# Gated stage: the next load of x ahead of the stores of prepared parts; first expert: units in pairs

## The chip, the core and the metric

The kernel runs on one core of a Trainium2 chip. The metric is the device time of one execution, in microseconds (us), as the median of several runs. The engines are TensorE (PE in the profile: matmuls; PEld: their weight loads), VectorE (DVE), ScalarE (ACT), GpSimd (POOL) and SyncE (SP), whose queue here issues all loads and stores of the stages that matter below.

## The reference

Three stages follow each other. Attention over keys and values that are averaged by eights gives x (2304 rows of 512). Four experts with relu, weighted by given probabilities, turn it into a new x. A gated block multiplies two projections, and two more matrices follow.

```python
k_p = k.reshape(B, H, Sp, 8, D).mean(axis=3)          # v_p likewise
attn = softmax(scale * q @ k_p.T)                     # exp, sum, divide
x = (attn @ v_p) as (2304, 512)
p = domain_probs / (domain_probs.sum(-1) + 1e-09)
for e in range(4):
    h = np.maximum(x @ w1[e], 0.0)                    # 512 -> 1024
    out += p[:, e:e + 1] * (h @ w2[e])                # 1024 -> 512
x = out
h = (x @ g_w1) * (x @ g_w2) @ g_w3
result = h @ g_wout
```

All of it is in float32.

## The kernel before, in words

Each product is made of three matmuls, since each operand is split into a rounded high part and the rest (`mm3`, lines 173 to 175; `hi_lo`, lines 178 and 179). Rounded means that ScalarE copies the operand into a type of fewer bits, and VectorE or GpSimd subtracts the copy from the operand.

**First expert.** It runs over six blocks of 384 rows and, in each, over eight slices of 128 hidden columns: 48 units. A unit has a first product (`expert_h`: x times w1, 12 matmuls of 384 columns into one PSUM bank, called F below) and a second product (h times w2, 9 matmuls of 512 columns into three banks, called S). Two banks alternate for first products (`g1_bank`). ScalarE applies the relu (line 688) and VectorE takes the rest (line 689), and these two hidden tiles sit in rings of `LAG + 1` places until the second product, `LAG` = 2 units later, has read them. The order of the work is the order in which this code is written: `run_units` writes F of unit n, a gap of attention pieces (`between(2 * n)`), S of unit n - 2, and another gap (`between(2 * n + 1)`). The pieces of the gaps (scores, exponentials, sums, normalisation, transposes, the product with v, loads) prepare x for the later blocks; which gap takes which piece is a table (`hooks`, `also`). The product with v (`attend`, line 557, tile x_ps) takes four banks, two of them the ones that alternate for first products.

**Gated stage.** It goes twice (`half`) over three batches of 768 rows. A batch has four rounds of seven products (`gated_rows`, `seven`: 168 matmuls of 384 columns, tile s) and then second products (72 matmuls of 512 columns, tile g). In the first half, while a batch runs, the x of the next batch is prepared (`prepare_x`): it is loaded into a buffer (`load_x`, line 775, tile xr, which lies in the area x5h), two ScalarE copies make high parts (lines 905 and 906), VectorE the rest and the sums, and at the end four stores per part are put on the list `stores` (line 918, to `kept`). `put_away` issues what is on that list. One buffer serves all these loads, so the load of the next x waits until the last preparation has read it. `give` copies a finished tile out of PSUM with ScalarE (line 1402) and stores it (line 1403, tile half). In the round that follows, ScalarE first makes the copies of the newly loaded x (`prepare_x(0, ...)`) and then copies the first of the seven products out of PSUM (line 961), on which VectorE's additions and the release of the banks depend.

Of the kernel before, what the change touches and what calls it, by code (L numbers as in the profile page):

```python
# [17 lines left out]
def fused_kernel(  # L18
# [23 lines left out]
    E, _, F = moe_w1.shape  # L42
    P = 128
# [8 lines left out]
    FC = F // P  # L52
# [16 lines left out]
    LAG = 2  # L69
# [41 lines left out]
    def row(base, at, size, bufs):  # L111
        return Ring(base, [at + size * n for n in range(bufs)])
# [13 lines left out]
    ZT = 2 * BS * 4  # L126
    XO = 7 * HALF_ROW
    EXTRA = 2 * P * 4
# [5 lines left out]
    H0 = 2 * FC * ROW  # L134
    HT = XT // KC

    def area(tag, size, dtype, name):
        return home.tile([P, size // 4], dtype, tag=tag, name=name)
# [3 lines left out]
    round_ = area("round", (FC - 1) * ZT + 2 * EXTRA, F32R, "round")  # L142
# [1 line left out]
    acc_a = Places(acc=Ring(plain, [WORK]))  # L144
    dp = plain[:, :NTILE * E].rearrange("p (t e) -> p t e", e=E)
    w1pool = Places(w1h=row(round_, 0, ROW, FC), w1l=row(round_, FC * ROW, ROW, FC))
    hpool = Places(hh=row(round_, H0, HT, LAG + 1), hl=row(round_, H0 + (LAG + 1) * HT, HT, LAG + 1))
    dpool = ctx.enter_context(tc.tile_pool(name="dpool", bufs=1, space=bass.MemoryType.DRAM))
    ps_q = ctx.enter_context(tc.tile_pool(name="ps_q", bufs=1, space=PSUM))
    ps_p = ctx.enter_context(tc.tile_pool(name="ps_p", bufs=KC, space=PSUM))  # L150
# [21 lines left out]
    def mm3(ps, lh, ll, rh, rl, first, last):  # L172
        nc.tensor.matmul(ps, lh, rl, start=first, stop=False)  # L173
        nc.tensor.matmul(ps, ll, rh, start=False, stop=False)  # L174
        nc.tensor.matmul(ps, lh, rh, start=False, stop=last)  # L175
# [62 lines left out]
    class Rounding:  # L238
# [35 lines left out]
        def step(self, most):  # L274
            self.load()
            if self.steps == most:
                self.flush()
                return
            self.steps += 1
            r, sink = self.loaded.pop(0)  # L280
            a = dec.tile([P, HALF], F32, tag="store")
            au = a.bitcast(U32)
            l, h = r[:, :, 0], r[:, :, 1]
            low = r.bitcast(F32)[:, :, 0]
            nc.vector.tensor_scalar(au, h, 0x7FFFFFFF, None, op0=ALU.bitwise_and)  # L285
            nc.vector.tensor_scalar(h, h, 0x80000000, None, op0=ALU.bitwise_and)
            nc.vector.tensor_scalar(a, a, LEAST, MOST, op0=ALU.max, op1=ALU.min)
            self.flush()
            nc.vector.scalar_tensor_tensor(au, au, 3, h, op0=ALU.logical_shift_left, op1=ALU.bitwise_xor)
            nc.vector.tensor_scalar(low, l, 2.0 ** -51, 2.0, op0=ALU.mult, op1=ALU.add)  # L290
            nc.gpsimd.tensor_tensor(au, au, l, op=ALU.add)  # L291
            self.done = a, sink
# [37 lines left out]
    with tc.manual_schedule():  # L330
# [60 lines left out]
        def cooled(most):  # L391
            while cooling and cooling[0][0] <= most:
                _, kind, spot = cooling.pop(0)
                spots[kind].append(spot)
# [180 lines left out]
        def fetch(most=None, only=None):  # L575
            for what in loads[:most]:
                if spots[kind_of(what)] and (only is None or what in only):
                    loads.remove(what)
                    {"q": load_q, "qb": load_qb, "k": load_k, "v": load_v}[what[0]](*what[1:])

        def do(piece):
            what, f = piece
            f()
            if what:
                done(what)
# [61 lines left out]
        at = {TPB: 0, TPB + 1: 5, TPB + 2: 8}  # L647
# [123 lines left out]
        def load_x(b, kc):  # L771
            r = late["small"].tile([P, 2, 2, HB], F32, tag="xr", name="xr", bufs=2)
            for n in range(2):
                rows = turned_d[(kc + 2 * n) * P:(kc + 2 * n + 1) * P]
                nc.sync.dma_start(r[:, n], rows[:, b * BS:(b + 1) * BS].rearrange("p (a s) -> p a s", a=2))
            xr_t[kc] = r
# [143 lines left out]
        def put_away():  # L920
            for f in stores:
                f()
            stores.clear()
# [64 lines left out]
        def between(n):  # L988
            clock[0] = n + 1
            cooled(n - 1)  # L990
            fetch(2)
            if n < len(hooks):
                for piece in hooks[n]:
                    do(piece)

        units = [("e", (0, i), fc) for i in range(NB) for fc in range(FC)]
        w_units = [("w", (b,), fc) for b in range(len(w3_blocks)) for fc in range(FC)]

        def make(u):
            kind, key, fc = u  # L1000
            return {"e": expert_h, "w": w3_h}[kind](*key, fc)

        def weights(u):
            kind, key, fc = u
            if kind == "e":
                return w2_t[key[0], fc]
            return wo_t[fc]

        def finish(u, pss):
            kind, key, fc = u  # L1010
            {"e": accumulate, "w": keep_w34}[kind](*key, pss)

        def rows(u):
            return w3_blocks[u[1][0]][1] if u[0] == "w" else TPB
# [3 lines left out]
        FIRST = ATT_BLOCKS * FC + 4  # L1018
        also = {}
# [24 lines left out]
        def made(u):  # L1044

            kind, key, fc = u
            if kind == "e":
                e, i = key
                if i == 0:
                    if fc + LAG < FC:  # L1050
                        stream.split(nc.vector)
                    stream.split()
            else:
                n = key[0] * FC + fc
                for f in early.get(n, ()):
                    f()
# [10 lines left out]
        def met(u):  # L1067

            kind, key, fc = u
            if kind == "e":  # L1070
                e, i = key
                if i == NB - 1:
                    stream.split()


        def add_pair(e, j):
            for fc in (j, j + NJ):
                stream.add(moe_w1[e, :, fc * P:(fc + 1) * P].rearrange("(k p) f -> p k f", p=P), (KC, P))

        def refill_first():  # L1080
            for n in range(FIRST, NB * FC + LAG):
                if n in at_pairs:
                    add_pair(1, at_pairs[n])
                if n >= NB * FC + LAG - FC:
                    add_w2(1, turn_of[n - (NB * FC + LAG - FC)])
            for j in range(len(at_pairs), NJ):
                add_pair(1, j)
# [36 lines left out]

        hs = {}

        def run_units(units, lo, hi):
            for n in range(lo, hi):
                if n < len(units):
                    u = units[n]  # L1130
                    hs[n] = make(u)
                    made(u)
                    if u[0] == "e":
                        if n == FIRST:
                            refill_first()
                        between(2 * n)
                        for f in also.get(2 * n, ()):
                            f()
                if n >= LAG:
                    u = units[n - LAG]  # L1140
                    fc = u[2]
                    if fc == 0:
                        n_out = rows(u)
                        pss[:] = [(bank_p if u[0] == "e" else bank_r)("g2") for _ in range(n_out)]
                    hh, hl = hs.pop(n - LAG)
                    wh, wl = weights(u)
                    for o, ps in enumerate(pss):
                        sl = slice(o * P, (o + 1) * P)
                        mm3(ps, hh[:, sl], hl[:, sl], wh[:, 0], wl[:, 0], fc == 0, fc == FC - 1)
                    if fc == FC - 1:  # L1150
                        finish(u, pss)
                    met(u)
                if n < len(units) and units[n][0] == "e":
                    between(2 * n + 1)
                    for f in also.get(2 * n + 1, ()):
                        f()

        pss = []
        run_units(units, 0, len(units) + LAG)

        def take_x():
            xo_t.update(xo_next)
# [174 lines left out]
        for half in range(2):  # L1337
            for n_b, b in enumerate(g_order):
# [3 lines left out]
                make = half == 0 and not swap  # L1342
# [77 lines left out]
                for m in range(len(tiles)):  # L1420
                    js = range(NJ) if last and m >= 2 else [NJ - 1]
                    if last and m == len(tiles) - 1:
                        for cols in pieces:
                            run(m, js, cols)
                            give_part(m, cols)
                        break
                    run(m, js)
                    give(m)
                    if swap and m == 2:
                        weights_of(2)  # L1430
                    if m == 1:
                        put_away()
                if half == 0 and n_b < BN - 2:
                    load_x(g_order[n_b + 2], 0)
                if not last:
                    spare_slot = second
                    take_x()
# [35 lines left out]
```

## Time and profile before

| | |
|---|---|
| median of 3 runs | 1164.74 us (1164.29 to 1164.87) |
| the profiled execution | 1164.62 us |
| its span, first to last instruction | 1162.9 us |
| PE busy | 1144.2 us, 98% of the span |
| PEld busy | 1035.3 us, 89% |
| DVE busy | 792.1 us, 68% |
| POOL busy | 423.5 us, 36% |
| ACT busy | 370.0 us, 32% |
| DMA, read and written | 213.85 MB, mean 184 GB/s |

The profile page also cuts the span into 40 equal slices of 29.07 us and gives the busy tenths of each engine in each, with the granted clock of TensorE. Where a slice of the busiest engine falls below 9 tenths, the chain of waits (the work that ended last, followed back step by step) says what it waited for. A timeline lists instructions in order of time; "x4" at the end of a row means that four were merged into it, and the bracket gives the idle time of the engine ahead of it and what ended that. SyncE's rows (SPq) show the time that issuing a DMA took, and not the transfer. A busy TensorE is not necessarily a fast one, so the start-to-start distance of matmuls is read as well.

### The profile page before, as it was taken

To read this page: it belongs to the slowest core of one execution; us is meant where nothing else is said; L and a number is where in the kernel's file an instruction comes from. 1 tells how busy PE (TensorE), PEld (TensorE's weight loads), DVE (VectorE), ACT (ScalarE), POOL (GpSimd) and SP (SyncE) were. 2 spreads that over 40 slices of the span, in tenths; PEclk is the share of its full clock that TensorE was granted. 3 is DMA by queue.
4 is the path that set the end of the run, shared out by engine and by line. 5 is a ranking of instruction groups with operands and counts; after the bars stand their busy time and mean duration, and the time that the engine had idled before them with its cause. 6 is when DMAs were issued, how large, how long until landed. Compare 5 with 4: busy or idle time off the path is not lost.

```text
span 1162.9 us, 17117 instructions
## 1 busy us (share of the span) xinstructions
PE 1144.2 (98%) x5966; PEld 1035.3 (89%) x5966; DVE 792.1 (68%) x1464; ACT 370.0 (32%) x615; POOL 423.5 (36%) x393
## 2 busy tenths in 40 slices
PE   8999999999999999999999999999999979999998
PEld 6888898999989898989898989899889979999997
DVE  6867553767768598748679568786786545774554
ACT  4543433345313053504043512225352213230110
POOL 6975212424615166624336643424001011331211
PEclk9999999999999999999999999999999989999999
DMA  8866424364876726496944588875475344947341
GB/s 220 198 155 144 159 83 163 153 196 177 293 246 188 237 78 184 145 293 201 261 135 118 169 258 201 244 180 179 120 182 203 143 156 176 340 167 269 120 168 55
DMA packets 213766, 213.85 MB, mean 184 GB/s; under 512 B 88880, under 2 KB 169008, under 8 KB 213680
## 3 DMA queue, kind: packets, MB, share of 16 engines
q1 hardware_dynamic: 213392, 212.23, 58.3%
q8 instruction: 47, 0.77, 0.3%
q10 hardware_dynamic: 288, 0.52, 0.1%
q14 instruction: 39, 0.32, 0.1%
HBM read 140.87 MB, written 71.83 MB: 183 GB/s over the span
## 4 chain that ended last, share of the span: by engine, by line
PE 90%; issue 3%; DMA 3%; DVE 2%; SPq 1%; ACT 1%; POOL 1%; POOLq 0%; DVEq 0%; ACTq 0%
PE g L174 17%; PE g L175 17%; PE g L173 17%; PE s L173 12%; PE s L175 12%; PE s L174 12%; PE x_ps L557 1%; PE sc L503 1%; DMA raw<-in_moe_w_dram 1%; PE at_ps L542 1%; POOL round L179 0%; DMA x5h<-turned 0%; SPq L1403 0%; DVE ap L418 0%; DMA plain<-gate 0%
## 5 line engine op out<-in xcount | busy, mean ns | idle before, releaser
L957 DVE TENSOR_TENSOR plain<-s,plain 128x384 f32<-128x384 f32 x300 | 158.2, 554 | 90.6 <-ACT plain L961 39.3
L179 POOL TENSOR_TENSOR round<-x5l,round 128x768 fp32r<-128x768 f32 x60 | 112.3, 1871 | 282.2 <-ACT round L178 247.8
L173 PE MATMUL s<-xo,wh 128*128 128x384 f32 x624 | 209.0, 335 | 0.0
L175 PE MATMUL s<-xo,wh 128*128 128x384 f32 x624 | 209.0, 335 | 0.0
L174 PE MATMUL s<-xo,wl 128*128 128x384 f32 x624 | 208.9, 335 | 0.0
L173 PE MATMUL g<-w2l,round 128*128 128x512 f32 x522 | 204.4, 392 | 0.0
L175 PE MATMUL g<-w2h,round 128*128 128x512 f32 x522 | 204.1, 391 | 0.0
L174 PE MATMUL g<-w2h,round 128*128 128x512 f32 x522 | 203.9, 391 | 0.0
L173 PEld LDWEIGHTS s<-xo,wh 128*128 128x128 f32 x624 | 117.6, 188 | 0.5
L174 PEld LDWEIGHTS s<-xo,wl 128*128 128x128 f32 x624 | 117.5, 188 | 0.5
L175 PEld LDWEIGHTS s<-xo,wh 128*128 128x128 f32 x624 | 117.4, 188 | 0.0
L175 PEld LDWEIGHTS g<-w2h,round 128*128 128x128 f32 x522 | 98.0, 188 | 20.7
L173 PEld LDWEIGHTS g<-w2l,round 128*128 128x128 f32 x522 | 98.1, 188 | 19.6 <-issue 0.8
L174 PEld LDWEIGHTS g<-w2h,round 128*128 128x128 f32 x522 | 98.0, 188 | 19.0
L291 POOL TENSOR_TENSOR x5l<-x5l,x5h 128x256 uint32<-128x256 uint32 x80 | 60.5, 757 | 139.6 <-DVE x5h L290 132.9
L961 ACT ACTIVATE plain<-s 128x384 f32<-128x384 f32 x60 | 29.2, 487 | 230.9 <-PE s L175 195.1
L178 ACT ACTIVATE round<-x5l 128x768 fp32r<-128x768 f32 x60 | 50.9, 848 | 146.1 <-DVE x5l L1332 145.0
L179 POOL TENSOR_TENSOR round<-plain,round 128x768 fp32r<-128x768 f32 (+1 forms) x29 | 52.3, 1805 | 115.3 <-ACT round L178 86.6
L285 DVE TENSOR_SCALAR x5l<-x5h 128x256 uint32<-128x256 uint32 x80 | 50.5, 632 | 54.7 <-DMA gate<-x5l 31.1
L957 DVE TENSOR_TENSOR x5l<-s,plain 128x384 f32<-128x384 f32 x120 | 65.2, 555 | 24.3 <-PE s L175 17.8
L689 DVE SCALAR_TENSOR_TENSOR round<-g,round 128x384 fp32r<-128x384 f32 x48 | 26.4, 553 | 62.9 <-ACT round L688 62.7
L173 PE MATMUL g<-xl,round 128*128 128x384 f32 x192 | 66.6, 347 | 0.0
(240 smaller groups left out, 2215.4 us busy)
## 6 DMA issues: line engine op xcount, KB each, us to landing
xo<-keptx SPq DMA_DIRECT2D x42, 768.0 KB
raw<-in_moe_w_dram SPq DMA_DIRECT2D x64, 256.0 KB
keptx<-xo SPq DMA_DIRECT2D x12, 768.0 KB
x5h<-in_moe_w_dram SPq DMA_DIRECT2D x128, 64.0 KB
x5h<-in_moe_w_dram SPq DMA_DIRECT2D x32, 256.0 KB
ob<-acc SPq DMA_DIRECT2D x24, 256.0 KB
kept<-xo SPq DMA_DIRECT2D x8, 768.0 KB
xo<-kept SPq DMA_DIRECT2D x8, 768.0 KB
```

Source lines behind the costliest of these rows:

```text
L173: nc.tensor.matmul(ps, lh, rl, start=first, stop=False)
L174: nc.tensor.matmul(ps, ll, rh, start=False, stop=False)
L175: nc.tensor.matmul(ps, lh, rh, start=False, stop=last)
L178: nc.scalar.activation(hi, src, AF.Copy)
L179: (lo_eng or nc.vector).tensor_tensor(lo, src, hi.bitcast(F32), op=ALU.subtract)
L285: nc.vector.tensor_scalar(au, h, 0x7FFFFFFF, None, op0=ALU.bitwise_and)
L291: nc.gpsimd.tensor_tensor(au, au, l, op=ALU.add)
L503: nc.tensor.matmul(sc[off:off + n, (hp % 2) * W:(hp % 2 + 1) * W], qT[:, hp, off:off + n], kT_t[b][:, hp * W:(hp + 1) * W], start=True, st ...
L542: nc.tensor.transpose(pt[:NK, g * P:(g + 1) * P], e[:, half * G + g, :], ident)
L689: nc.vector.scalar_tensor_tensor(hl, ps, 0.0, hh.bitcast(F32), op0=ALU.max, op1=ALU.subtract)
L957: nc.vector.tensor_tensor(to, one, two, op=ALU.add)
L961: nc.scalar.activation(x, product(j, A11, B11), AF.Copy)
```

## The change

In the gated stage, `put_away` is no longer called after the second finished tile of a batch but after all six, and behind the load of x for the batch after the next one. In the first expert the first eight units run as before; from the ninth on, two units go together: two first products, then two second products, with the same numbered gaps behind each of the four. The rings of hidden tiles have four places in place of three. The rest of `run_units` serves the later weight products as before.

```diff
-    hpool = Places(hh=row(round_, H0, HT, LAG + 1), hl=row(round_, H0 + (LAG + 1) * HT, HT, LAG + 1))
+    hpool = Places(hh=row(round_, H0, HT, LAG + 2), hl=row(round_, H0 + (LAG + 2) * HT, HT, LAG + 2))
...
+        def begin_unit(units, n):
+            if n < len(units):
+                u = units[n]
+                hs[n] = make(u)
+                made(u)
+
+        def end_unit(units, n):
...
         def run_units(units, lo, hi):
             for n in range(lo, hi):
...
+                begin_unit(units, n)
+                end_unit(units, n - LAG)
+
+        def run_first():
+
+            def gap(at):
+                if at >= 2 * len(units):
+                    return
+                between(at)
+                for f in also.get(at, ()):
+                    f()
+
+            n, total = 0, len(units) + LAG
+            while n < total:
+                few = 1 if n < FC else 2
+                if n == FIRST:
+                    refill_first()
+                steps = [lambda m=m: begin_unit(units, m) for m in range(n, n + few)]
+                steps += [lambda m=m: end_unit(units, m - LAG) for m in range(n, n + few)]
+                for k, step in enumerate(steps):
+                    step()
+                    gap(2 * n + k)
+                n += few
...
-        run_units(units, 0, len(units) + LAG)
+        run_first()
...
-                    if m == 1:
-                        put_away()
                 if half == 0 and n_b < BN - 2:
                     load_x(g_order[n_b + 2], 0)
+                put_away()
```

On SyncE, at the end of the first gated batch: before, seven of the eight stores of prepared parts (kept), four of the six finished tiles (half), and the load of x (x5h from turned; the row merges it with the batch's later load).

```order
L918 DMA kept<-round 128x1536
L918 DMA kept<-round 128x1152
L918 DMA kept<-z_2637 128x1536
L918 DMA kept<-xo 128x1152
L918 DMA kept<-xo 128x1536
L918 DMA kept<-xo 128x1152
L918 DMA kept<-xo 128x1536
L1403 DMA half_8070<-ob 128x512
L1403 DMA half_8071<-ob 128x512
L1403 DMA half_8072<-ob 128x512
L1403 DMA half_8073<-ob 128x512
L775 DMA x5h<-turned 128x768 x4
```

On SyncE at the same place in the changed kernel (its lines are numbered one to nineteen higher).

```order
L1422 DMA half_8069<-plain 128x512
L1422 DMA half_8070<-ob 128x512
L1422 DMA half_8071<-ob 128x512
L1422 DMA half_8072<-ob 128x512
L1422 DMA half_8073<-ob 128x512
L776 DMA x5h<-turned 128x768 x2
L919 DMA kept<-round 128x1152
L919 DMA kept<-round 128x1536
L919 DMA kept<-round 128x1152
L919 DMA kept<-z_2637 128x1536
```

The load of x stands ahead of all eight stores, and so do the four half stores that stood behind them.

On TensorE, between units 46 and 47 of the first expert (g1 is the bank of a first product, g2 those of a second one): before, the end of one first product, a second product, and the beginning of the next first one.

```order
L175 MATMUL g1_2524<-xh_1910,round_71 128x384
L173 MATMUL g2_2390<-w2l_635,round_71 128x512
L174 MATMUL g2_2390<-w2h_634,round_71 128x512
L175 MATMUL g2_2390<-w2h_634,round_71 128x512
L173 MATMUL g2_2391<-w2l_635,round_71 128x512
L174 MATMUL g2_2391<-w2h_634,round_71 128x512
L175 MATMUL g2_2391<-w2h_634,round_71 128x512
L173 MATMUL g2_2392<-w2l_635,round_71 128x512
L174 MATMUL g2_2392<-w2h_634,round_71 128x512
L175 MATMUL g2_2392<-w2h_634,round_71 128x512
L173 MATMUL g1_2556<-xl_1911,round_71 128x384
```

On TensorE in the changed kernel, from the end of the first of these first products (g1_2540 is the second one).

```order
L174 MATMUL g1_2524<-xl_1911,round_71 128x384
L175 MATMUL g1_2524<-xh_1910,round_71 128x384
L176 MATMUL g1_2524<-xh_1910,round_71 128x384
L174 MATMUL g1_2540<-xl_1911,round_71 128x384
L175 MATMUL g1_2540<-xh_1910,round_71 128x384
L176 MATMUL g1_2540<-xh_1910,round_71 128x384
```

The second product has moved behind the next first product, where it is followed by another second product.

On TensorE, at the product with v for the third block (x_ps, gap 24) and the scores (sc) behind it: before.

```order
L557 MATMUL x_ps_1128<-ap1_72 64x384 x2
L557 MATMUL x_ps_1133<-ap1_72 64x384 x2
L557 MATMUL x_ps_1138<-ap1_72 64x384 x2
L557 MATMUL x_ps_1143<-ap1_72 64x384 x2
L503 MATMUL sc_1148<-ap1_72 128x144 x2
L503 MATMUL sc_1151<-ap1_72 128x144 x2
L173 MATMUL g2_1029<-w2l_505,round_71 128x512
```

On TensorE at the same gap in the changed kernel.

```order
L558 MATMUL x_ps_1128<-ap1_72 64x384 x2
L558 MATMUL x_ps_1133<-ap1_72 64x384 x2
L558 MATMUL x_ps_1138<-ap1_72 64x384 x2
L558 MATMUL x_ps_1143<-ap1_72 64x384 x2
L504 MATMUL sc_1148<-ap1_72 128x144 x2
L504 MATMUL sc_1151<-ap1_72 128x144 x2
L174 MATMUL g1_1160<-xl_814,round_71 128x384
```

A first product now follows the attention pieces where a second product followed; it writes one of the two banks that the x_ps pieces have just used.

## Rows read from the trace of the kernel before

**Rows 1.** Page, busy tenths of TensorE in 40 slices of the span.
```profile
PE   8999999999999999999999999999999979999998
```

**Rows 2.** Chain that ended last, 920 to 960: start us, us, what.
```profile
937.87 5.38 DMA x5h<-turned
...
944.02 0.48 ACT plain L961
```

**Rows 3.** Stretches: us, PE, PEld, DVE, ACT, POOL busy (x), PEclk, DMA share, GB/s.
```profile
875.59:904.73 29.14, 29.14 (x169) 29.14 (x168) 21.08 (x36) 6.03 (x11) 5.73 (x3) 1.00 0.39 161
...
921.10:960.52 39.42, 31.76 (x169) 31.44 (x168) 20.71 (x35) 7.90 (x15) 5.72 (x3) 0.87 0.52 200
```

**Rows 4.** Timeline of TensorE at 944: start us, us, instruction [idle before, releaser].
```profile
944.55 0.69 PE L173 MATMUL s<-z,wh 128*128 128x384 f32 x1 [7.66 <-ACT plain L961]
```

**Rows 5.** Waits of TensorE, 25 to 275: us in total, times, longest us.
```profile
PE kT_ps L431 <- POOL plain L423: 1.1, 2, 0.6
PE sc L503 <- DVE ap L490: 0.8, 1, 0.8
```

**Rows 6.** Timeline of SyncE's queue, 911 to 968: start us, us, DMAs issued.
```profile
911.00 0.80 SPq L775 DMA_DIRECT2D x5h<-turned  x2
921.16 0.81 SPq L1403 DMA_DIRECT2D half<-plain  x2
922.02 2.17 SPq L918 DMA_DIRECT2D kept<-round  x3
...
931.45 5.10 SPq L1403 DMA_DIRECT2D half<-ob  x4
936.60 30.98 SPq L775 DMA_DIRECT2D x5h<-turned  x4
```

**Rows 7.** Timeline of VectorE at 920, the buffer's last reader.
```profile
920.68 1.76 DVE L179 TENSOR_TENSOR xo<-x5h,xo 128x1536 fp32r<-128x1536 f32 x1 [1.56 <-ACT xo L178]
```

**Rows 8.** Timeline of ScalarE, 915 to 944.
```profile
915.04 0.85 ACT L906 ACTIVATE xo<-x5h 128x768 fp32r<-128x768 f32 x1 [0.47 <-DMA x5h<-turned]
...
921.51 2.07 ACT L1402 ACTIVATE ob<-g 128x512 f32<-128x512 f32 x4
...
930.25 0.85 ACT L178 ACTIVATE round<-x5l 128x768 fp32r<-128x768 f32 x1 [6.29 <-DVE x5l L1332]
942.43 0.52 ACT L905 ACTIVATE xo<-x5h 128x384 fp32r<-128x384 f32 x1 [11.34 <-DMA x5h<-turned]
943.27 0.84 ACT L906 ACTIVATE xo<-x5h 128x768 fp32r<-128x768 f32 x1 [0.33 <-DMA x5h<-turned]
```

**Rows 9.** Timeline of TensorE at the first expert's end, first matmul of each product.
```profile
266.70 0.33 PE L173 MATMUL g<-xl,round 128*128 128x384 f32 x1
...
268.80 0.39 PE L173 MATMUL g<-w2l,round 128*128 128x512 f32 x1
...
270.88 0.39 PE L173 MATMUL g<-w2l,round 128*128 128x512 f32 x1
...
272.92 0.39 PE L173 MATMUL g<-w2l,round 128*128 128x512 f32 x1
```

**Rows 10.** Timeline of VectorE behind the x_ps pieces of the third block.
```profile
95.95 2.50 DVE L179 TENSOR_TENSOR xl<-x_ps,xh 128x384 fp32r<-128x384 f32 x4 [0.21 <-ACT xh L178]
```

**Rows 11.** Timeline of TensorE beside attention: a second product, and a transpose of weights.
```profile
98.21 0.49 PE L173 MATMUL g<-w2l,round 128*128 128x512 f32 x1
...
110.61 1.04 PE L542 MATMUL at_ps<-ident,ap 128*72 128x128 f32 x8
```

**Rows 12.** Timeline of GpSimd at 104, the normalisation.
```profile
104.56 1.15 POOL L533 TENSOR_TENSOR ap<-ap 128x576 f32<-128x576 f32 x1
```

**Rows 13.** Stretches of the first expert, columns as in rows 3.
```profile
100.00:110.00 10.00, 10.00 (x59) 9.23 (x58) 9.73 (x17) 3.29 (x7) 5.77 (x12) 1.00 0.22 62
110.00:120.00 10.00, 10.00 (x62) 9.24 (x61) 4.13 (x9) 3.58 (x8) 8.89 (x17) 1.00 0.46 107
```

More of the change, by code (lines that the diff above doesn't have):

```diff
@@ L146, in fused_kernel @@
     w1pool = Places(w1h=row(round_, 0, ROW, FC), w1l=row(round_, FC * ROW, ROW, FC))
-    hpool = Places(hh=row(round_, H0, HT, LAG + 1), hl=row(round_, H0 + (LAG + 1) * HT, HT, LAG + 1))
+    hpool = Places(hh=row(round_, H0, HT, LAG + 2), hl=row(round_, H0 + (LAG + 2) * HT, HT, LAG + 2))
+    assert H0 + 2 * (LAG + 2) * HT <= (FC - 1) * ZT + 2 * EXTRA
     dpool = ctx.enter_context(tc.tile_pool(name="dpool", bufs=1, space=bass.MemoryType.DRAM))
@@ L1125, in fused_kernel @@
         hs = {}
+        def begin_unit(units, n):
[4 more added lines that the diff above has]
+        def end_unit(units, n):
+            if n < 0:
+                return
+            u = units[n]
+            fc = u[2]
+            if fc == 0:
+                n_out = rows(u)
+                pss[:] = [(bank_p if u[0] == "e" else bank_r)("g2") for _ in range(n_out)]
+            hh, hl = hs.pop(n)
+            wh, wl = weights(u)
+            for o, ps in enumerate(pss):
+                sl = slice(o * P, (o + 1) * P)
+                mm3(ps, hh[:, sl], hl[:, sl], wh[:, 0], wl[:, 0], fc == 0, fc == FC - 1)
+            if fc == FC - 1:
+                finish(u, pss)
+            met(u)
@@ L1127, in run_units @@
         def run_units(units, lo, hi):
             for n in range(lo, hi):
[L1129 to L1156, printed above, removed]
+                begin_unit(units, n)
[3 more added lines that the diff above has]
+                if at >= 2 * len(units):
+                    return
+                between(at)
[12 more added lines that the diff above has]
+                n += few
```

## Prediction

> **What bounds the kernel now.** I read the page's busy slices first, for TensorE: 9 tenths or more in nearly every slice, with one 7, the 33rd (930 to 959 us) [rows 1]. So TensorE sets the pace, and a change counts only where it alters TensorE's idle time or the pace of its matmuls. The chain of waits in that slice leaves TensorE [rows 2]: it runs through a transfer of x that starts at 937.87 and takes 5.38 us, and the copy on ScalarE at line 961, behind which the next product waits. The stretches say what this costs [rows 3]: the 168 matmuls of first products of a gated batch take 29.14 us in the first batch (875.59 to 904.73), but 39.42 us in the second, from 921.10. That is 10.28 us lost in one place. Its parts: TensorE stood idle for 7.66 us before the matmul at 944.55 [rows 4], and the mean granted clock of the second batch is 0.87 against 1.00 [rows 3], because after that idle stretch the clock fell to its lower level for a while. In the first expert, TensorE's largest waits between 25 and 275 us are 1.1 and 0.8 us in all [rows 5]; what can be gained there is pace, not waiting.
>
> **Part one: the load of x goes ahead of the stores.** In the first gated batch SyncE's queue runs in this order [rows 6]: a load of x at 911.00, two half stores at 921.16, eight stores of prepared parts from 922.02, four half stores at 931.45, and at 936.60 the load for the next batch. The queue is slow there: two half stores took 0.81 us to issue before the eight, four took 5.10 us behind them. The changed order puts six half stores and the load first and the eight stores behind them; every one of these DMAs is still issued.
>
> When does the load start? It needs its buffer free: the last reader is VectorE's subtraction at 920.68, which ends at 922.44 [rows 7]. It needs the half stores ahead of it issued: the ScalarE copies that fill them end at 921.51 + 2.07 = 923.58 [rows 8], and one issue then costs some 0.4 us. So I put the load's first issue at about 924.0, 12.6 us earlier than now. When does it land? The load issued at 911.00 behind nothing let ScalarE's second copy of x start at 915.04 [rows 8], 4.0 us later; the load of 936.60, issued behind twelve stores, let it start at 943.27, 6.7 us later. These are my two bounds; six half stores stand ahead of it, so I take the worse one: data at 930.7. When is it needed? ScalarE splits the last hidden rows at 930.25 for 0.85 us [rows 8] and reaches the copies of x at 931.1, so the load is no longer what it waits for. The two copies and the copy at line 961 take 0.52 + 0.84 + 0.48 = 1.84 us [rows 2, 8]; TensorE, which ran on without them to 944.55 - 7.66 = 936.9, runs dry only if the data comes after about 935. That leaves 4 us of cover. If the cover went, each us past 935 would cost a us, and the slow clock on top.
>
> What is late next? The stores: they now issue from about 925 and, at 1.28 us a piece (5.10 / 4), are through by 936. The next entry behind them is the batch's other load of x. In the trace it is the second half of the group of four at 936.60 that lasts 30.98 us, to 967.6 [rows 6]: it waits for its buffer, and the stores are gone 20 us before, even with the batch 10 us earlier. In the second batch no load of x stands behind the stores, only the gate loads for weights that are made one batch later. So part one gives the whole 10.28 us, with nothing behind it that takes some back.
>
> **Part two: units in pairs.** Nothing is added or removed on any engine; from the ninth unit on, the order F S F S (a first product, a second product) becomes F F S S. The attention pieces stay at the same count of products. What a change of kind costs can be read at the end of this expert, where second products follow each other [rows 9]: the one right behind a first product takes 270.88 - 268.80 = 2.08 us, the next 272.92 - 270.88 = 2.04. So F to S costs 0.04. A first product behind a second takes 268.80 - 266.70 = 2.10; 12 matmuls at the pace of the long run of the same width (29.14 / 168 = 0.1735 [rows 3]) take 2.08. So S to F costs 0.02. Counting along TensorE's order, direct F to S goes from 32 places to 14, S to F from 26 to 14: 18 x 0.04 + 12 x 0.02 = 0.96 us gained. Where an attention piece lies between, only the kind of its neighbour changes; I cost that at nothing, and let it be 0.5 either way.
>
> These rows bear on a statement of the notes. The Trainium skill (TensorE: Matmul & The Clock Gate, section Back-to-back issue gap) gives the gap of isolated matmuls as columns / 2.4 + 2.5 ns, a function of the width alone, so the order of kinds would not matter. The trace disagrees: 231 ns against 227 for the same width, by the kind of product before it. By the page part two would give nothing, and the time would be that of the first rival below.
>
> Three things could take the 0.96 back. (a) PSUM banks: two alternate for first products. Behind the attention's four x_ps pieces, the second F of a pair now follows where an S stood, and takes the bank that the third piece leaves. In the trace the four subtractions that free them run from 95.95 to 98.45 [rows 10], and the following product starts at 98.21 [rows 11]; the third ends near 97.8. No wait; at worst 0.24 us, at two places. (b) VectorE: the second F's subtraction (line 689) now stands ahead of one gap of attention pieces, which must wait for that product, about 2 us. The tightest user I found is the normalisation on GpSimd at 104.56 for 1.15 [rows 12], which TensorE uses at 110.61 [rows 11]: 4.9 us of room, so it is covered; if it were not, it would cost at most the 2 us. (c) The buffers of hidden rows grow from three to four, so no new wait comes from them. Bounds of part two: from a gain of 0.96 + 0.5 to a loss of 0.48 + 2; I take 0.96, since the rows nearest to it are the products themselves.
>
> **Sum.** The profiled execution took 1164.62 us (span 1162.9 and 1.7 around it), 0.12 under the median of 1164.74. 1164.62 - 10.28 - 0.96 = 1153.38; plus 0.12 for the median: 1153.5.
>
> **Rivals.**
> 1. Part one works and the pairs give nothing, or lose a little to (a) and (b): 1154.5, up to 1156.0. For it: the 0.04 is read at the resolution of a hundredth, and attention work fills the first half of the pairs. Against: the products on both sides of it show the same 2.10 and 2.08.
> 2. The wait at 944.55 stays in part, because the load, though ahead, starts late (the queue waits for the sixth half store's ScalarE copy), or because its transfer shares the DMA engines with the half stores and the eight stores behind. Half of it left: 1158.6; all of it: 1163.8. Against: 4 us of cover beyond the worse of two measured landings.
> 3. Slower: the pairs starve TensorE while VectorE carries the attention. VectorE is busy 9.73 of 10 us at 100 to 110 [rows 13], and its order now makes attention pieces wait behind the second subtraction of each pair. If the lateness adds up from pair to pair instead of being worked off, the next first product finds its PSUM bank still full. It decides once a bank is not free three products (some 6.3 us) after it was filled. Twelve pairs lie beside attention; 2 us late in each, as in (b), is 24 us, so 1153.5 + 24 + 1.0 (no gain from pairs) = 1178.5. To come out slower than before it must lose over 11.2 us in all. Against: in 110 to 120 VectorE is busy 4.13 us only [rows 13], so a debt of 2 us is paid within a pair or two.
>
> **How the numbers follow.** Forecast 0.72; rival 1 0.15; rival 2 0.09 (two thirds of it still well faster, one third so near the old time that it counts as the same); rival 3 0.04. Differences under 0.2% (2.3 us) can't be told from none. Faster: 0.72 + 0.15 + 0.06 = 0.93; same 0.03; slower 0.04. The range takes in the forecast with part two's best (1153.5 - 0.5, and 0.6 for the spread of single runs, which was 0.58 before) and all of rival 1: 1152.4 to 1156.0, leaving about 0.13 outside.
>
> **What the changed profile would show.** Right: no slice below 9 in the gated stage; the second batch's first products in 29.1 to 29.2 us at granted clock 1.00; ScalarE's first copy of x there directly behind the split, not behind a DMA; the eight stores issued after the load. In the first expert: the second products of a pair at 2.08 and 2.04, and its end about 1 us earlier. Wrong: an idle stretch of TensorE at that batch, or waits of TensorE for VectorE or GpSimd between 70 and 180 us that rows 5 do not have. A gated stage as before with a shorter first expert, or the reverse, would say which part carried the difference.

## The result, and the profile after

The changed kernel takes 1155.3 us (median of 4 runs, 1154.23 to 1156.08) where the kernel before, beside it, takes 1164.6 (1164.29 to 1164.87): a ratio of 0.992, 95% interval 0.9902 to 0.9937. That is 9.3 us faster. The forecast was 1153.5, with 1152.4 to 1156.0 as its range. The profiled execution took 1155.34 us (span 1153.6), 9.28 less than that of before.

The page's busy slices of the changed kernel, which answer to [rows 1]: TensorE's busy tenths, and its granted clock.

```profile
PE   8999999999999999999999999999999999999998
...
PEclk8999999999999999999999999999999999999999
```

The 7 of the 33rd slice is gone. The stretches of the first products of the three gated batches that a load or a store touches say the same; the columns are those of [rows 3].

```profile
876.39:905.54 29.15, 29.15 (x170) 29.14 (x168) 21.07 (x36) 6.04 (x11) 5.72 (x3) 1.00 0.39 159
921.90:951.21 29.31, 29.31 (x169) 29.10 (x168) 21.28 (x35) 7.92 (x15) 5.72 (x3) 1.00 0.70 269
967.57:996.79 29.22, 29.22 (x169) 29.12 (x168) 19.04 (x31) 6.66 (x13) 5.54 (x3) 1.00 1.00 367
```

The second batch's 168 products took 39.42 us and take 29.31 (10.11 gained), at a granted clock of 1.00 in place of 0.87. DMA moves 269 GB/s instead of 200 there: the same bytes, in a stretch that is 10.11 us shorter. The queue of SyncE in the changed kernel, which answers to [rows 6] (start us, us, DMAs issued):

```profile
922.20 0.81 SPq L1422 DMA_DIRECT2D half<-plain  x2
923.18 2.11 SPq L1422 DMA_DIRECT2D half<-ob  x4
925.38 1.54 SPq L776 DMA_DIRECT2D x5h<-turned  x2
926.98 2.08 SPq L919 DMA_DIRECT2D kept<-round  x3
...
930.65 4.89 SPq L919 DMA_DIRECT2D kept<-xo  x4
957.47 0.80 SPq L776 DMA_DIRECT2D x5h<-turned  x2
```

And ScalarE's timeline there, which answers to the last rows of [rows 8]:

```profile
931.22 0.85 ACT L179 ACTIVATE round<-x5l 128x768 fp32r<-128x768 f32 x1 [6.22 <-DVE x5l L1351]
931.97 0.51 ACT L906 ACTIVATE xo<-x5h 128x384 fp32r<-128x384 f32 x1
932.38 0.83 ACT L907 ACTIVATE xo<-x5h 128x768 fp32r<-128x768 f32 x1
933.12 0.47 ACT L962 ACTIVATE plain<-s 128x384 f32<-128x384 f32 x1
```

The copies of x (L906, L907) follow the split with no bracket: the 11.34 us of idle time that ended at a DMA are gone.

The first expert did not become shorter. From the ninth unit's first product to the first product of the next expert (tile s), the kernel before and the changed one show, on TensorE:

```profile
70.46 0.34 PE L173 MATMUL g<-xl,round 128*128 128x384 f32 x1
...
274.96 0.33 PE L173 MATMUL s<-xo,wh 128*128 128x384 f32 x1
```

```profile
70.80 0.34 PE L174 MATMUL g<-xl,round 128*128 128x384 f32 x1
...
240.42 0.45 PE L174 MATMUL g<-xl,round 128*128 128x384 f32 x1 [1.10 <-DVE round L690]
...
275.76 0.33 PE L174 MATMUL s<-xo,wh 128*128 128x384 f32 x1
```

That is 204.50 us before and 204.96 after: 0.46 lost, where 0.96 was to be gained. A new wait stands at 240.42, which [rows 5] do not have. The ledger of the two traces, start to start: up to the ninth unit, where the order of the work is the same, +0.34; the paired units +0.46; the second gated batch -10.11; all the rest together +0.02. The sum is -9.29, the 9.28 above but for rounding.

### The profile page after: what moved, and what is told of

It is laid out like the page before. It is cut to its first block, busy times and chain, and to the rows that moved or that the text cites. A ratio compares the mean times of both kernels' runs of the same rounds, so it can differ in the third digit from the quotient of the medians.

```text
span 1153.6 us, 17118 instructions
## 1 busy us (share of the span) xinstructions
PE 1140.9 (99%) x5966; PEld 1032.6 (90%) x5966; DVE 795.5 (69%) x1464; ACT 369.9 (32%) x615; POOL 422.5 (37%) x393
## 4 chain that ended last, share of the span: by engine, by line
PE 90%; issue 3%; DMA 2%; DVE 2%; POOL 1%; ACT 1%; SPq 1%; POOLq 0%; ACTq 0%; DVEq 0%
PE g L175 17%; PE g L174 17%; PE g L176 17%; PE s L174 12%; PE s L175 12%; PE s L176 12%; PE sc L504 1%; PE x_ps L558 1%; PE at_ps L543 1%; DMA raw<-in_moe_w_dram 1%; POOL round L180 1%; DMA stxl<-in_k_dram 0%; DMA plain<-gate 0%; DVE wl L180 0%; SPq L1263 0%
## 5 line engine op out<-in xcount | busy, mean ns | idle before, releaser
L1189 ACT ACTIVATE plain<-plain 128x768 f32<-128x768 f32 x36 | 30.6, 849 | 110.4 <-DVE plain L958 110.4
```

The source lines that it names most:

```text
L1189: nc.scalar.activation(r, r, AF.Relu)
```

## The experiments

Each was run beside the kernel before on its chip; that took 1164.46 (15 runs) for the first four, 1164.73 (9 runs) for the next four and 1164.74 (9 runs) for the last three.

**e1_load_first: the gated part alone.**

```diff
-                    if m == 1:
-                        put_away()
                 if half == 0 and n_b < BN - 2:
                     load_x(g_order[n_b + 2], 0)
+                put_away()
```

> The kernel before with the gated stage's change alone (six half stores, the load of x, then the eight stores); units of the first expert singly. My theory: the second gated batch's first products fall from 39.4 to about 29.3 us, and the median from 1164.6 to about 1154.5 (10.1 less). Rival (the pairs carry part of the difference): less than 9 us gained.

Measured: 1153.99 us (4 runs), ratio 0.9912 (0.9897 to 0.9927). Its first expert takes 204.50 us as before; its second batch, columns as above:

```profile
920.19:949.44 29.25, 29.25 (x169) 29.09 (x168) 21.23 (x35) 7.87 (x15) 5.72 (x3) 1.00 0.70 270
```

Part one alone is worth all of the gain.

**e2_pairs_only: the pairs alone.** The changed kernel with the gated stage of before.

```diff
+                    if m == 1:
+                        put_away()
                 if half == 0 and n_b < BN - 2:
                     load_x(g_order[n_b + 2], 0)
-                put_away()
```

> The changed kernel with the gated stage of before: only the pairs are left. My theory: fewer changes of kind save 0.94 us, and one wait of a first product for its bank, near 240 us, costs 1.4: about 1165.1, 0.3 to 0.7 slower than before. Rival one (the late transfer of weights was chance, the order has no part in it): no such wait, 1163.7. Rival two (pairs change nothing): 1164.6.

Measured: 1164.91 us (11 runs), ratio 1.0004 (0.9995 to 1.0013). The medians can't tell a loss of 0.46 us from none; the trace can. The paired units take 204.97 us, and the wait is there without the gated change; the waits of TensorE from 25 to 275 us (us in total, times, longest) begin with it:

```profile
PE g L174 <- DVE round L690: 1.1, 1, 1.1
```

So the pairs bring the wait, and as they stand they gain nothing. Where it comes from is read in the changed kernel's trace, first on ScalarE, then on VectorE:

```profile
236.48 0.63 ACT L179 ACTIVATE wh<-raw 128x512 fp32r<-128x512 f32 x1 [4.88 <-DMA raw<-in_moe_w_dram]
...
237.66 0.47 ACT L689 ACTIVATE round<-g 128x384 fp32r<-128x384 f32 x1
```

```profile
238.88 1.02 DVE L180 TENSOR_TENSOR wl<-raw,wh 128x512 fp32r<-128x512 f32 x2
239.82 0.55 DVE L690 SCALAR_TENSOR_TENSOR round<-g,round 128x384 fp32r<-128x384 f32 x1
```

In gaps 76 and 77 the weights of the next expert are split; ScalarE waits 4.88 us there for their raw load, and unit 39's relu (237.66) and subtraction (239.82) stand behind the pieces of gap 76 on their engines. That subtraction frees the bank that unit 41's first product, the one at 240.42, writes. In the order of before, unit 41's first product starts behind unit 38's second product; in pairs it starts behind unit 40's first one, which follows unit 37's second product: one second product, 2.1 us, earlier. The pair of first products in which it lies takes 5.59 us where an undisturbed one takes 4.19: 1.40 lost. In the kernel before, the same transfer lets ScalarE start at 235.94, and unit 39's subtraction is the first of the two merged in this row of VectorE:

```profile
240.48 1.01 DVE L689 SCALAR_TENSOR_TENSOR round<-g,round 128x384 fp32r<-128x384 f32 x2
```

It ends at about 240.48 + 0.55 = 241.03, and unit 41's first product starts at 241.58: 0.55 us to spare, where the pairs ask for 2.1. Why the raw load is late stands in SyncE's queue of the changed kernel:

```profile
215.09 16.26 SPq L819 DMA_DIRECT2D keptx<-xo  x4
231.41 1.49 SPq L200 DMA_DIRECT2D raw<-in_moe_w_dram  x2
```

It is queued behind stores that wait for their data, close to the arrangement that part one mended in the gated stage, a load behind stores.

**e3_weights_later: the changed kernel, unit 38's weight pieces behind the pair's second products.**

```diff
-                also.setdefault(2 * n + part, []).append(lambda j=j, part=part: weights_of(j, part))
+                also.setdefault(2 * n + 2 * (n % 2 == 0) + part, []).append(lambda j=j, part=part: weights_of(j, part))
```

> The changed kernel with the preparation of the first pair of expert weights, at unit 38, put behind the pair's two second products instead of between and behind its two first products. My theory: VectorE takes unit 39's subtraction before the weights' work, the wait of TensorE near 240 us goes, and the median falls from 1155.3 by 1.4 to about 1153.9. Rival (the wait only moves to a later unit, or comes from the transfer alone): 1155.3 again.

Measured: 1154.1 us (4 runs), ratio 0.9913 (0.9899 to 0.9926). The wait is gone, and the paired units take 203.56 us, 0.94 less than before:

```profile
70.85 0.34 PE L174 MATMUL g<-xl,round 128*128 128x384 f32 x1
...
274.41 0.33 PE L174 MATMUL s<-xo,wh 128*128 128x384 f32 x1
```

With the wait taken away, the pairs give what the sum had for them.

**e4_load_last: six half stores, then the stores, then the load.** The kernel before with `put_away()` moved behind the six half stores but left ahead of the load.

```diff
-                    if m == 1:
-                        put_away()
+                put_away()
                 if half == 0 and n_b < BN - 2:
                     load_x(g_order[n_b + 2], 0)
```

> The kernel before with the eight stores moved behind all six half stores, but the load of x still behind the stores. My theory: only the place of the load against the stores counts, so the second gated batch's first products take 39 us or a little more, as before, and the time is 1164 to 1166. Rival (what held the queue was the half stores waiting behind the stores): about 29.3 us there and 1154.5.

Measured: 1164.57 us in one run. The row of the second batch, columns as above:

```profile
920.69:960.09 39.40, 31.71 (x170) 31.23 (x168) 20.81 (x35) 8.09 (x15) 5.72 (x3) 0.87 0.53 200
```

The place of the half stores is worth nothing; the load's place against the eight stores is worth all. The load itself, on SyncE, and ScalarE's second copy of x:

```profile
933.55 33.59 SPq L775 DMA_DIRECT2D x5h<-turned  x4
```

```profile
943.03 0.84 ACT L906 ACTIVATE xo<-x5h 128x768 fp32r<-128x768 f32 x1 [0.36 <-DMA x5h<-turned]
```

Counted from the batch's start, the load issues 2.6 us sooner than before (933.55 - 920.69 = 12.9 us against 936.60 - 921.10 = 15.5), and the second copy still starts at the same time (22.3 us against 22.2). From issue to copy it takes 9.5 us here. So the earlier issue alone bought nothing: with the same stores ahead of it, the data came when it had come before. In the kernel before, DMA is busy 0.96 of the time from 921 to 937, at 381 GB/s; that the load waits for this traffic fits, and is not shown more directly.

**e5_load_amid: four stores, the load, four stores.**

```diff
-                    if m == 1:
-                        put_away()
+                for f in stores[:4]:
+                    f()
+                del stores[:4]
                 if half == 0 and n_b < BN - 2:
                     load_x(g_order[n_b + 2], 0)
+                put_away()
```

> The kernel before with six half stores first, then four of the eight stores, the load of x, and the other four stores. My theory (4 us of cover, lost at the rate at which the queue issues): the load issues some 4.5 us later than with no store ahead and lands 6.7 us after that, near 936, about 1 us past the point where TensorE runs dry: the second gated batch's first products take 30 to 31 us. Rival (landing follows the shorter of the two measured times, so four stores are still covered): 29.3 us. Second rival (any store ahead costs its whole share of the old loss): half of 10.1, 34 us.

Measured: 1158.66 us in one run. Its SyncE queue, its ScalarE, and TensorE where it waited:

```profile
928.30 2.45 SPq L775 DMA_DIRECT2D x5h<-turned  x2
```

```profile
936.75 0.52 ACT L905 ACTIVATE xo<-x5h 128x384 fp32r<-128x384 f32 x1 [5.74 <-DMA x5h<-turned]
937.71 0.84 ACT L906 ACTIVATE xo<-x5h 128x768 fp32r<-128x768 f32 x1 [0.44 <-DMA x5h<-turned]
```

```profile
938.99 0.44 PE L173 MATMUL s<-z,wh 128*128 128x384 f32 x1 [2.18 <-ACT plain L961]
```

The second copy starts 9.4 us after the load's issue, more than both of my bounds (4.0 and 6.7). TensorE ran dry at 938.99 - 2.18 = 936.81; the prediction had 936.9. The second batch takes 31.65 us, 2.40 more than in e1_load_first, of which 2.18 are this wait; the third waits another 1.3 for VectorE. The granted clock of the second batch stayed at 1.00, so the slow clock that the prediction put on top of such a wait did not come with it. In the kernel before, behind 7.66 idle us, it was 0.53 from 944.50 to 950.00, near the lower of its two levels.

**e6_mixed: first and second products mixed, three matmuls at a time, in units 30 to 47** (with the gated part of e1_load_first).

```diff
...
+            for kc in range(KC):
+                mm3(ps, wh[:, kc, :], wl[:, kc, :], xh[:, kc, :], xl[:, kc, :], kc == 0, kc == KC - 1)
+                if kc < TPB:
+                    sl = slice(kc * P, (kc + 1) * P)
+                    mm3(pss[kc], ph[:, sl], pl[:, sl], vh[:, 0], vl[:, 0], v[2] == 0, v[2] == FC - 1)
...
```

> The load-first kernel with single units, in which units 30 to 47 of the first expert mix the two products three matmuls at a time: three changes from F to S and three back per unit in place of one each, with the same matmuls. If a change of kind costs a fixed 0.04 and 0.02 us (as my sum had it): 4.31 us per unit in place of 4.19, 2.2 us more over 18 units. Rival (not the change is slow but the nine or so matmuls that follow it): every S as slow as now and every F at 0.178, 4.22 us per unit, 0.5 us more in all.

Measured: 1165.04 us in one run, with waits for ScalarE and VectorE elsewhere in the first expert that the mixing brought, so its total says nothing on pace. An undisturbed unit does (TensorE, first matmul of a unit's first group of second products):

```profile
222.95 0.39 PE L173 MATMUL g<-w2l,round 128*128 128x512 f32 x1
...
227.16 0.39 PE L173 MATMUL g<-w2l,round 128*128 128x512 f32 x1
```

4.21 us, where a unit of before takes 4.185. It changes kind six times where a unit of before changes twice. At a fixed 0.04 and 0.02 for each change it would take 4.185 + 2 x 0.06 = 4.305. The pair in the changed trace shows what holds instead (TensorE, a pair's first products from 212.13, its second products from 216.32):

```profile
212.13 0.33 PE L174 MATMUL g<-xl,round 128*128 128x384 f32 x1
...
213.20 0.33 PE L174 MATMUL g<-xl,round 128*128 128x384 f32 x1
...
216.32 0.39 PE L174 MATMUL g<-w2l,round 128*128 128x512 f32 x1
...
218.40 0.39 PE L174 MATMUL g<-w2l,round 128*128 128x512 f32 x1
...
220.44 0.33 PE L174 MATMUL g<-xl,round 128*128 128x384 f32 x1
```

The first six matmuls of the pair's first products go at 1.07 / 6 = 0.178 us, the other 18 at 3.12 / 18 = 0.173; the first nine of its second products at 2.08 / 9 = 0.231, the next nine at 2.04 / 9 = 0.227. It is a slower pace of the first matmuls behind a change, so a shorter run pays it for all of them: 12 x 0.178 + 9 x 0.231 = 4.22, against the 4.21 measured. What in TensorE makes it was not settled.

**e7_fill_early: the changed kernel, with the next expert's raw weights asked for earlier.** The loads go into SyncE's queue ahead of the stores that wait, 184.81 us into the span.

```diff
                 if n == FIRST:
                     refill_first()
+                    stream.fill()
```

> The changed kernel with one call more: the four first loads of the next expert's weights are issued when they are put on the list (unit 28), in place of when the first is taken, where they stand on SyncE's queue behind stores of x's sums that wait some 15 us. My theory: the wait of TensorE near 240 us comes from this late transfer together with the pair order, so it goes without touching the order; the median falls by 1.4 from 1155.3, to about 1153.9. Rival (the order alone makes it: the second subtraction stands behind the weights' work whenever that starts): the wait of 1.1 us stays, 1155.3.

Measured: 1153.77 us (5 runs), ratio 0.9911 (0.9898 to 0.9925). The wait is gone; ScalarE splits the weights at 230.07, with no bracket:

```profile
230.07 0.93 ACT L179 ACTIVATE wh<-raw 128x512 fp32r<-128x512 f32 x2
```

The paired units take 203.56 us (69.38 to 272.94). Two different remedies, one of the place of the weight pieces and one of their data, give the same 203.56; so the wait came from both together, and 1.40 is its price.

**e8_stores_pool: the stores on GpSimd's queue.** The kernel before, with the eight stores issued on GpSimd's queue at their old place in the code, so that no load stands behind them in a queue.

```diff
...
             for f in stores:
-                f()
+                f(nc.gpsimd)
             stores.clear()
...
```

> The kernel before with the eight stores left at their old place in the program but issued on GpSimd's queue, so that the half stores and the load of x no longer stand behind them on SyncE's. If the queue order made the loss: the load issues near 925, the second gated batch's first products take 29 to 30 us, about 1154.5. Rival (the DMA engines were the limit: 381 GB/s at a share of 0.96, whoever issues): the load shares them with the stores, lands a few us before 943, and the batch keeps more than half of the loss, 35 us or more.

Measured: 1169.78 us in one run, slower than before. GpSimd issues some stores as soon as their data are there, 13 us earlier than SyncE did [rows 6], and they meet the load of x that SyncE issues at 910.73 (GpSimd, then ScalarE):

```profile
909.03 1.80 POOL L918 DMA_DIRECT2D kept<-round  x3
```

```profile
917.88 0.53 ACT L905 ACTIVATE xo<-x5h 128x384 fp32r<-128x384 f32 x1 [9.08 <-DMA x5h<-turned]
```

From 908 to 921 us DMA moves 272 GB/s here, at a share of 0.73, and 61 at 0.17 in the kernel before. The second copy of x starts 9.8 us after the issue (920.53), against 4.0 before [rows 6, 8], so the prepared operand is late and TensorE waits in two batches (waits from 920 to 1015):

```profile
PE s L173 <- DVE z L179: 5.5, 1, 5.5
PE s L173 <- DVE xo L179: 5.4, 1, 5.4
```

A queue of its own for the stores, at their old place in the code, is thus no remedy: the load must be ahead of their traffic in time, not only in its queue. Stores on GpSimd's queue but issued later were not tried.

**Three versions side by side, on one chip.** The changed kernel, e1 and e7, unaltered, since the medians above come from several chips.

> The changed kernel once more, beside two others on the same chip. Theory (the pairs gain 0.94 us of pace and lose 1.40 us to the wait behind the weight pieces): it lies 0.46 us above the kernel with the load first and no pairs, and 1.4 us above the changed kernel that fills the weight stream earlier. Rival (what stands between the medians 1155.3, 1153.99 and 1153.77 is the lead before the ninth unit, which differs by up to 1.4 us from run to run): no order between the three that the spread does not cover.

> The kernel before with the load of x ahead of the stores and no pairs. Theory: 10.3 to 10.5 us under before, and 0.46 us under the changed kernel, 0.94 us over the one that fills earlier. Rival: the three cannot be told apart.

> The changed kernel with the weight stream filled at unit FIRST. Theory: 1.4 us under the changed kernel and 0.94 us under the load alone, so about 11.3 us under before. Rival: not to be told from the load alone, since the lead differs by more than 0.94 us from run to run.

| | us (lowest to highest, runs) | ratio to before (95%) | paired or plain units, from the trace |
|---|---|---|---|
| changed kernel | 1154.29 (1154.18 to 1154.5, 5) | 0.9913 (0.9899 to 0.9927) | 204.92 |
| load first, no pairs | 1153.57 (1153.38 to 1154.59, 4) | 0.9908 (0.9895 to 0.9922) | 204.50 |
| pairs, weights asked for earlier | 1153.24 (1152.51 to 1153.92, 4) | 0.9903 (0.9890 to 0.9917) | 203.56 |

The order is the theory's; the distances between the medians, 0.72 and 0.33 us, are not its 0.46 and 0.94. The third lies 1.05 us under the changed kernel, and their runs do not overlap; its median is the lowest of the three. The load alone can be told from neither by its runs. The ninth unit begins between 69.38 and 70.85 in the traces of the experiments, and what follows the first expert differs again by up to 0.6 us (span less the start of the next expert: 877.46 in the changed kernel, 878.05 in the third). Both are of the size of the terms at stake. So the 0.94 is shown for the paired units, from start to start, and not in the time of the whole kernel.

## Why the prediction came out as it did

**Part one: right, in mechanism and size.** 10.28 was forecast; the trace shows 10.11, and e1_load_first 10.47 by medians. The load was to issue at 924.0; the changed trace stands 0.80 later at the first gated batch, so 924.8, and it is 925.38: the copies that fill the half stores end at 922.55 + 2.06 = 924.61, 0.23 later than the shift makes them, and the load issues 0.77 us behind them, not 0.4. ScalarE did not wait for it. The step on stores that issue behind it also held: they are out by 930.65 + 4.89 = 935.54 (forecast 936), and the next load only goes at 957.47. That the 936 came out so close is luck: they start at 926.98, not at 925, and take 8.56 / 8 = 1.07 us a piece, not 1.28.

**The landing bounds: too narrow as a bound, harmless here.** I called 6.7 us the worse landing. e5_load_amid shows 9.4, e4_load_last 9.5 and e8_stores_pool 9.8 where stores are moving. In the changed kernel the second copy starts at 932.38 without a wait, at most 7.0 us after the issue. My estimate: a landing of 9.8 would have brought the data at 935.2, and TensorE needed it by about 935.8 (my 935, shifted by 0.80), which is 0.6 us of cover where I claimed 4. Rival 2 is thus a real mechanism at another place in the queue; e5 paid its price, 31.65 against 29.25 in e1_load_first. I had set the landing at a fixed time behind the issue. e4_load_last shows that it is not: the load issued sooner behind the same stores, and its data came no sooner.

**Part two, pace: right in size, too simple in form.** 0.96 was forecast; 0.94 shows in e3, e7 and e11 alike. As a cost for each change it holds for whole groups only; e6_mixed refutes it below that. The Trainium skill (TensorE: Matmul & The Clock Gate, section Back-to-back issue gap) gives the gap of isolated matmuls by the width alone, and says itself that in a stream the weight loads set the spacing too. So "by the page part two would give nothing" took it for more than it states. In the stream of this trace the width alone does not set the gap: 0.231 and 0.227 us at 512 columns, 0.178 and 0.173 at 384, in one stretch at granted clock 1.00.

**Part two, what takes it back: this step failed.** It looked for a late bank (a) only where x_ps takes one, and for a late VectorE (b) only where attention pieces stand, with 4.9 us of room at the tightest. The wait came where neither looked: a bank that VectorE frees late behind weight pieces of the next expert, which wait for a load. The order of before got through there with 0.55 us to spare. I had read TensorE's waits up to 275 us and found none to add to, and had not asked which places came close to one. The 1.40 it cost made a gain of 0.94 into a loss of 0.46: the result is rival 1, "the pairs give nothing, or lose a little to (a) and (b)". Its form was right, its place not named. The median stayed inside the range because the range took in all of that rival, not because the sum held.

**The x_ps banks, (c) and rival 3: not seen.** TensorE's other waits between 25 and 275 us are those of [rows 5] to a tenth:

```profile
PE kT_ps L432 <- POOL plain L424: 1.1, 2, 0.6
PE sc L504 <- DVE ap L491: 0.8, 1, 0.8
```

No lateness adds up over the pairs beside attention; VectorE is busy 8.83 of 10 us in 100 to 110 and 5.37 in the next ten, 14.20 together against 13.86 in [rows 13].

**The rest.** The sum had 1153.38 for the profiled execution, which took 1155.34, 1.96 more. Of these, 1.40 is the wait, 0.34 the lead before the ninth unit, 0.17 what part one fell short (10.28 - 10.11), and 0.05 is left, 0.02 of it the pace. On the chip of the last three runs the changed kernel took 1154.29.

## What to carry to other kernels

A load that the pace depends on belongs ahead, in time, of the stores that nobody waits for; another queue did not replace that here. When the order of work changes, search the trace not only for waits but for places that come within a few tenths of one, above all where an engine in between waits for a transfer: the margin there is to be set against how much earlier the new order asks. A term under the spread of runs is to be read from start to start in a trace, and tested by taking away what cancels it.

## What the runs showed of the hardware that I had not expected

- Behind a change of product kind the next six to nine matmuls go slower by some 2 to 3% (0.231 against 0.227 us, 0.178 against 0.173). It is no fixed sum per change: that would make a mixed unit 4.305 us, and it takes 4.21.
- A load's landing (from its issue to the second copy of x) depends on the stores in motion around it: 4.0 us alone, at most 7.0 behind six half stores, 6.7 behind twelve stores, 9.5 when it is issued sooner behind the same stores, 9.4 between four and four, 9.8 beside four on another queue.
- Issuing half of the same stores some 13 us earlier, from GpSimd, made the kernel slower by about 5 us (one run, 1169.78 against 1164.73 beside it).
